# A fused windowed-attention, Fourier-mix and MLP kernel: 1/std moved behind the MLP, the first v loaded in 512-byte runs, the x bounce on ScalarE's DMA queue, w2 loaded at another point

## The chip, the cores and the metric

The kernel runs on one core of one Trainium2 chip. A time is the device time of one execution in microseconds (us); the median of several executions is compared. The engines of the core work beside each other, each through its own instructions in a fixed order, and wait for one another by semaphores: TensorE (PE; its weight loads are listed as PEld), VectorE (DVE), ScalarE (ACT), GpSimd (POOL) and SyncE (SP). A DMA is issued by one of SP, ACT or POOL as an instruction in that engine's order.

## The reference, cut to what matters

```python
# attention: q, k, v of (4 batches, 8 heads, 768 positions, 64)
scores = q @ k.T / 8 + bias                  # bias: minus slope of the head x distance
keep = is_global | is_local                  # the first 8 positions, and the last 96 up to here
a = exp(scores - max) over keep;  a = a / (sum(a) + 1e-9)
x = a @ v                                    # heads side by side: (4, 768, 512)
# mix and MLP
u = x + real(fft(fft(x, axis=1), axis=2))
mu, var = mean(u, -1), mean((u - mu)**2, -1)
un = (u - mu) / sqrt(var + 1e-6)
out = u + maximum(un @ w1, 0) @ w2           # w1 (512, 2048), w2 (2048, 512)
```

All inputs and the output are float32. A positive factor of a row passes through the maximum: maximum(s * un @ w1, 0) @ w2 is s times the value without s.

## The kernel before, in words

**Stages of a batch.** The four batches run one after the other, overlapped. For a batch, the heads are taken in four pairs (hp 0 to 3). q and k of a pair are loaded in float32 (`load`, `qk_dma`, L342), cast to float16 (`cast_qk`, L353 on ACT, L355 on DVE, L357 on POOL), transposed on TensorE (`trans`, L397) and copied out of PSUM (`qkT`, L403). `score` makes the scores of two blocks of 128 keys at a time (L437) and ACT takes the exponential. In batch 0 the distance bias is added in PSUM by a matmul with `sid` (the identity times -8 slope, made on POOL, L964), and the exponential is final (`ex`, L463). From batch 1 on the exponential (`er`, L460) is multiplied by a mask `mk` on DVE (L475); `mk` is made once, by 8 ACT steps (L957). v is loaded in float32 (L317) and cast into `v16` by POOL (`cast_v`, L368). `v_global` and `glob` (L486, L511) serve the 8 global keys. `av` multiplies with v (L547, L560), and DVE divides by the sum (L579, L580), which gives x.

**How v lies.** `v16` has partition p of a block hold the position 2m + t, where p = 64 t + m: the even positions in the lower half and the odd ones in the upper. v is therefore loaded by two DMAs, one for each t, in runs of one position: 64 floats, 256 bytes. q and k are loaded in runs of two positions, 512 bytes, by one DMA over all 128 partitions.

**The bounce.** The Fourier part along the positions wants x in two layouts: the one in which attention leaves it, and one with six adjacent positions in a partition, which is added to the mix to make u. The second comes by way of DRAM (`bounce`): two halves of x are written to `xd` (L598, two DMAs each) and read back as `xr` (L605, L606). All are issued by SP.

**Mix.** DVE folds x (`fold_s`, `fold_d`, L623 to L692), TensorE makes `py` (L712, L715), ACT or DVE copies it to `zy` (L728, L730), POOL mirrors part of it (L748 to L761), TensorE makes `pu` (L792). A batch has three row pairs of 2 x 128 rows (c = 3 b + 0, 1, 2). For each, DVE adds `pu` and `xr` to u (L809), takes the statistics (L818, L820), POOL makes 1/std and -mean/std (L825 to L828), ACT or DVE makes un (L838, L840), TensorE transposes it (L856) and ACT or DVE copies it to `unT` (L864, L866).

**MLP.** For each c, 8 groups `ph` (8 matmuls each, L884), evacuated with the maximum by ACT or DVE (L890, L891), and two outputs of 4 parts `pg` (L907, 4 matmuls each). DVE adds u (L918), SP stores (L922). PSUM has two buffers for `ph`, two for `pg` and two for everything else (batch 0 has two more, `C` and `D`, before the MLP's exist).

**The order of the work.** The order on each engine is fixed when the kernel is built, by a planner (class `Plan`). Each step is handed to it (`later`) with the engines that may do it and a cost for each, the names of what it needs, a latency, and a rank that decides between steps that could start at the same time. The planner keeps a clock for each engine and one for DMA, and takes what could start first; TensorE's units come from four streams (mix, attention, ph, pg), with ten units looked ahead in the first two. On the chip only true data dependencies are waited for: a need that is no data dependency (such as the `gate` in `load`, which holds the loads of batch 1 until `xr` of batch 0) shapes the order, and nothing else.

**Weights.** w1 and w2 are loaded as float16 by four POOL DMAs each (`wload`, L989, L992), w1 after the third v cast, w2 after the first 1/std in the planner's order.

Of the kernel before, what the change touches and what calls it, by code (L numbers as in the profile page):

```python
# [14 lines left out]
P = 128  # L15


class Plan:
# [9 lines left out]
    def __init__(self):  # L28
        self.t = {"PE": 0.0, "ACT": 0.0, "DVE": 0.0, "POOL": 0.0, "SP": 0.0, "DMA": 6.0}
        self.tok = {}  # L30
        self.ready = []
        self.pending = []
        self.rings = {}
        self.left = {}
        self.n = 0
# [49 lines left out]
    def emit(self, place):  # L85
# [6 lines left out]
        if dma:  # L92
            end = self.t["DMA"] = max(self.t["DMA"], end) + dma
# [78 lines left out]
def kernel(  # L172
# [132 lines left out]
    def load(b, hp, which):  # L305
# [4 lines left out]
        gate = [("xr", 0)] if HP <= n < HP + 4 else []  # L310
        if which == "v":
# [32 lines left out]
    def cast_qk(b, hp, w, src, freed):  # L344
# [14 lines left out]
        if b:  # L359
            ways = [("ACT", act(768), lambda: cast("ACT")), ("POOL", 1.6, lambda: cast("POOL"))]  # L360
        pl.later(ways, [("ld", "qk", n, w)] + free("qk", n), 0.0, [("qk", n, w)], [("free",) + freed],
                 rank=1 if b else 0)

# [12 lines left out]
    pl.users(("CD",), 3 * HP + 4 + 3 * NP + len(YG) + NP)  # L376
# [11 lines left out]
    def trans(b, hp):  # L388
        n = HP * b + hp

        def run(start, ring):
# [12 lines left out]
            pl.later([("DVE", dve2(2 * S), evac)], free("qkT", n), e, [("qkT", n)], ring=ring, rank=RA(b))  # L404
# [10 lines left out]
    def score(b, hp, g):  # L415
        n = HP * b + hp
        idx = 3 * (n - HP) + g
# [63 lines left out]
    def v_global(b, halves):  # L481
# [15 lines left out]
        ATT.append(([("v", b, 2 * half + i) for half in halves for i in range(2)] + [("one", 0)], BANKS(b), run))  # L497
# [34 lines left out]
    def av(b, part, jp):  # L532
# [4 lines left out]
        needs += [("v", b, hp) for hp in part]  # L537
# [51 lines left out]
    def bounce(b):  # L589

        for half in range(2):
            def wr(half=half):
# [4 lines left out]
                for t in range(2):  # L597
                    nc.sync.dma_start(rows[t], X[b][64 * t:64 * t + 64, :, c])  # L598
            pl.later([("SP", 0.9, wr)], [("x", b, hp, jp) for hp in (2 * half, 2 * half + 1) for jp in range(NP)] + [("xw", b, 0)][:half], 0.0,
                     [("xw", b, half)], [("free", "x", b)], lat=1.6, dma=2.0)  # L600

        def rd():
            XR[b] = buf("xr", b, [P, NS, Dm], FP16, 3)
            rows = XD[b].rearrange("(m r) d -> m r d", r=6)
            nc.sync.dma_start(XR[b][:, 0:3], rows[:, 0:3])  # L605
            nc.sync.dma_start(XR[b][:, 3:6], rows[:, 3:6])  # L606
        pl.later([("SP", 0.9, rd)], [("xw", b, 0), ("xw", b, 1)] + free("xr", b), 0.0, [("xr", b)], lat=1.6, dma=3.0)
# [170 lines left out]
    MV = {}  # L778
    UNT = {}

    def u_unit(b, pr):
# [4 lines left out]
        def run(start, ring):  # L786
# [20 lines left out]
            def add():  # L807
                u = UT[c] = buf("u", HP + c, [P, 2, Dm], FP32, 2)
                VT(u.rearrange("p a (n r) -> p a n r", r=4), pu.rearrange("p a (r n) -> p a n r", r=4),  # L809
                   XR[b][:, r0:r1 + 1:r1 - r0, :].rearrange("p a (n r) -> p a n r", r=4), op=ALU.add)  # L810
# [280 lines left out]
```

## Time and profile before

| | |
|---|---|
| median of three runs | 302.56 us (302.5 to 303.51) |
| profiled execution | 302.04 us, span 299.9 us |
| busy in the span: PE, DVE, ACT, POOL | 268.0, 183.3, 137.3, 65.8 us |
| mean granted clock of TensorE | 0.952 |
| DMA moved | 37.03 MB, of 66089 packets 26640 under 512 B |
| bounce writes, issue to landing | 2.9 to 10.1 us, median 3.8 |
| first v, issue to landing | 4.9 to 7.7 us, median 6.5 |

A line of the trace names the line of the kernel, the engine, the operation and the tiles that it writes and reads. "Idle before" is time in which that engine did nothing ahead of the instruction, and the releaser is what ended it. A stretch is read together with its clock: matmuls at a granted clock of 0.6 take longer, and the busy time of TensorE then holds less work. SPq and POOLq are the issue of DMAs by these engines.

### The profile page before, as it was taken

The page shows a single profiled execution, that of the slowest core. Times are in us where ns is not written, and L with a number is a line of the kernel's source. Part 1 is how long each engine was busy: PE and PEld are TensorE (multiplying, and loading weights), DVE is VectorE, ACT ScalarE, POOL GpSimd, SP SyncE. Part 2 cuts the span into 40 slices and gives each one's busy share as a digit, 9 for nine tenths or more (in the row PEclk, how much of TensorE's full clock was granted, in tenths as well). Part 3 has the DMA queues.
Part 4 walks back from the last instruction along what each step waited for, and adds up shares of the span by engine and source line. Part 5 has one row for each costly group of instructions (what it writes and reads, how often), then busy time and mean ns, then how long its engine had stood idle before and what let it go on. Part 6 is the DMA issues. An engine that isn't in the chain of part 4 may idle for free.

```text
span 299.9 us, 5827 instructions
## 1 busy us (share of the span) xinstructions
PE 268.0 (89%) x2388; PEld 174.3 (58%) x2388; DVE 183.3 (61%) x350; ACT 137.3 (46%) x189; POOL 65.8 (22%) x151
## 2 busy tenths in 40 slices
PE   2996474899999999559999999999999999999994
PEld 2353353586765546348678565686567758767541
DVE  1476879757556895874667958865688675100111
ACT  2388333675882233176745434658234135434100
POOL 3643015901212137151001125300000431000000
PEclk9999669599999999759999999999999999999998
DMA  8999969999799999330304511100053110100111
GB/s 191 236 229 205 267 201 206 218 217 221 142 214 221 196 264 240 134 107 8 99 0 106 188 42 37 71 2 0 3 142 124 48 39 35 37 1 36 70 70 70
DMA packets 66089, 37.03 MB, mean 123 GB/s; under 512 B 26640, under 2 KB 61712, under 8 KB 66064
## 3 DMA queue, kind: packets, MB, share of 16 engines
q1 hardware_dynamic: 61840, 32.48, 46.1%
q0 software_dynamic: 4224, 4.19, 8.5%
q8 instruction: 18, 0.29, 0.5%
q14 instruction: 7, 0.06, 0.1%
HBM read 31.42 MB, written 9.44 MB: 136 GB/s over the span
## 4 chain that ended last, share of the span: by engine, by line
PE 66%; DVE 12%; DMA 10%; SPq 6%; ACT 2%; POOL 1%; issue 1%; POOLq 0%; DVEq 0%
PE ph L884 26%; PE pg L907 23%; DMA qs<-in_k_dram 5%; PE pav L560 4%; PE sc L437 3%; SPq L317 3%; DMA u<-in_v_dram 2%; DMA xr<-xd 2%; PE pu L792 2%; PE pav L547 2%; SPq L342 2%; PE py L712 2%; DVE st L818 2%; PE ptu L856 2%; DVE u L809 2%; PE pt L397 1%
## 5 line engine op out<-in xcount | busy, mean ns | idle before, releaser
L884 PE MATMUL ph<-unT,w 128*128 128x256 f16 x768 | 97.6, 278 | 1.1 <-ACT unT L864 1.1
L907 PE MATMUL pg<-w,hT 128*128 128x512 f16 x384 | 90.8, 380 | 0.0
L884 PEld LDWEIGHTS <-w 128*128 128x128 f16 x768 | 72.8, 99 | 18.6 <-issue 6.5
L890 ACT ACTIVATE hT<-ph 128x512 f16<-128x512 f32 x69 | 41.2, 597 | 54.5 <-PE ph L884 54.4
L907 PEld LDWEIGHTS <-hT 128*128 128x128 f16 x384 | 36.2, 98 | 35.8 <-issue 1.1
L460 ACT ACTIVATE er<-sc 128x992 f16<-128x992 f32 (+2 forms) x36 | 33.0, 921 | 18.1 <-PE sc L437 11.6
L918 DVE TENSOR_TENSOR ob<-pg,u 128x512 f32<-128x512 f32 x24 | 16.5, 689 | 39.5 <-PE pg L907 37.8
L891 DVE TENSOR_SCALAR hT<-ph 128x512 f16<-128x512 f32 x27 | 18.7, 691 | 22.7 <-PE ph L884 22.5
L353 ACT ACTIVATE qk<-qs 128x768 f16<-128x768 f32 x23 | 18.8, 839 | 19.7 <-PE pt L397 7.9
L475 DVE TENSOR_TENSOR ex<-er,mk 128x992 f16<-128x992 f16 (+2 forms) x36 | 22.4, 635 | 4.1 <-ACT er L460 4.1
L761 POOL COPY ww<-zy 128x512 f16<-128x512 f16 x16 | 9.3, 612 | 54.6 <-PE py L712 37.5
L437 PE MATMUL sc<-qkT 64*128 64x256 f16 (+1 forms) x192 | 19.0, 282 | 0.6 <-DVE qkT L403 0.5
L728 ACT ACTIVATE zy<-py 128x512 f16<-128x512 f32 (+1 forms) x12 | 9.6, 810 | 20.3 <-PE py L715 17.5
L403 DVE COPY qkT<-pt 128x1536 f16<-128x1536 f16 x16 | 15.2, 950 | 5.7 <-PE pt L397 5.7
L838 ACT ACTIVATE un<-u,rstd 128x512 f16<-128x512 f32 x15 | 11.7, 809 | 15.1 <-POOL rstd L828 15.1
L560 PE MATMUL pav<-v,ex 128*128 128x65 f16 x352 | 18.3, 196 | 0.2 <-ACT er L460 0.2
L408 POOL COPY kG<-qkT 64x8 f16<-64x8 f16 x32 | 8.8, 276 | 41.0 <-DVE qkT L403 40.0
L397 PE MATMUL pt<-ident,qk 128*128 128x128 f16 x192 | 15.6, 236 | 2.4 <-ACT qk L353 1.4
L580 DVE TENSOR_TENSOR x<-pav,rc 128x512 f16<-128x512 f32 (+1 forms) x27 | 17.1, 632 | 0.9
L712 PE MATMUL py<-t,ww 128*128 128x256 f16 x48 | 11.7, 298 | 6.1 <-DVE ww L677 5.7
L809 DVE TENSOR_TENSOR u<-pu,xr 128x1024 f32<-128x1024 f32 x12 | 14.5, 1216 | 3.8 <-PE pu L792 3.7
L560 PEld LDWEIGHTS <-ex 128*128 128x128 f16 x352 | 13.3, 98 | 5.3 <-issue 0.6
(87 smaller groups left out, 283.9 us busy)
## 6 DMA issues: line engine op xcount, KB each, us to landing
out_dram<-ob SPq DMA_DIRECT2D x24, 256.0 KB, 2.0
qs<-in_q_dram SPq DMA_DIRECT2D x13, 384.0 KB, 6.6
qs<-in_k_dram SPq DMA_DIRECT2D x13, 384.0 KB, 6.5
vs<-in_v_dram SPq DMA_DIRECT2D x24, 192.0 KB, 7.1
w<-in_moe_w_ch_dram POOLq DMA_DIRECT2D x8, 512.0 KB, 10.3
xd<-x SPq DMA_DIRECT2D x16, 192.0 KB, 3.9
xr<-xd SPq DMA_DIRECT2D x8, 384.0 KB, 3.8
u<-in_v_dram SPq DMA_DIRECT2D x8, 192.0 KB, 6.5
```

The source lines that it names most:

```text
L353: A(d, s, AF.Copy)
L397: nc.tensor.transpose(o[:, j % 2], src[:, w, j].rearrange("p h d -> p (h d)"), idn)
L437: nc.tensor.matmul(pa[:, s, c0:c0 + cw], TT[n][lo:lo + 64, 1, i * P:(i + 1) * P], TT[n][lo:lo + 64, 0, i * P:i * P + cw], start=(b > 0), s ...
L460: A(mine(), cut(pa), AF.Exp, 0.0, 0.125)
L475: VT(o, mine(), m, op=ALU.mult)
L560: nc.tensor.matmul(po[:, jj, hh * 65:(hh + 1) * 65], lhsT, v16[b % 2][:, i, h, 0:65], start=(jp == 0 and a == 0), stop=(a == len(ops) - 1) ...
L712: nc.tensor.matmul(o, wr, t1_sb[:, rs, 128:384], start=True, stop=(wi is None))
L809: VT(u.rearrange("p a (n r) -> p a n r", r=4), pu.rearrange("p a (r n) -> p a n r", r=4), XR[b][:, r0:r1 + 1:r1 - r0, :].rearrange("p a (n ...
L884: nc.tensor.matmul(ph[:, a * CH:(a + 1) * CH], w1[:, d, jb * P:(jb + 1) * P], UNT[c][:, d, :], start=(d == 0), stop=(d == ND - 1))
L890: pl.later([("ACT", act(512), lambda: A(dst, ph, AF.Relu)), ("DVE", dve(512), lambda: V.tensor_scalar_max(dst, ph, 0.0))], [], e, [("h", c ...
L891: ("DVE", dve(512), lambda: V.tensor_scalar_max(dst, ph, 0.0))],
L907: nc.tensor.matmul(pg, HT[c][:, jb, t * P:(t + 1) * P], w2[:, jb, :], start=(jb == 0), stop=(jb == NJ - 1))
```

## The change: what it does, and the diff

Five things are changed together.

- **Normalisation.** u is made by two scalar_tensor_tensor steps of 512 columns, each of which also gives the sum of its row; a small DVE step makes -mean/16 of it. un becomes (u - mean)/16, without 1/std. ACT squares un and sums the squares; POOL makes 1/std (with the factor 16) from that in two steps. The last sum becomes `pg` x (16/std) + u. bn_stats, bn_aggr and two of POOL's four steps go.
- **First v.** The v of batch 0 is loaded like q and k, one DMA in runs of 512 bytes. It is cast to float16 (POOL, DVE or ACT) into a buffer of the `er` tag, and 12 matmuls of 64 x 64 blocks of the identity (`v_place`) put even and odd positions where `v16` wants them; two copies for each head pair (ACT or DVE) bring it there.
- **Bounce.** All writes and reads of the bounce are issued by ACT; the read is one DMA instead of two. The loads of batch 1 get the first write of batch 0's second half as their gate instead of `xr`.
- **Order.** The planner's clocks start otherwise and have a second DMA clock for ACT; `mk` is made after the last x of batch 0; `sid` is made by DVE; casts of batch 0 may go to POOL and `qkT` copies of batch 0 to ACT.
- **Weights.** w1 follows the last k of batch 0, w2 the second v of batch 1, in the planner's order.

```diff
-        self.t = {"PE": 0.0, "ACT": 0.0, "DVE": 0.0, "POOL": 0.0, "SP": 0.0, "DMA": 6.0}
+        self.t = {"PE": 0.0, "ACT": 0.0, "DVE": 0.0, "POOL": 0.0, "SP": 0.7, "DMA": 1.5, "DMA2": 0.0}
...
-            end = self.t["DMA"] = max(self.t["DMA"], end) + dma
+            q = "DMA2" if eng == "ACT" else "DMA"
+            end = self.t[q] = max(self.t[q], end) + dma
...
-        gate = [("xr", 0)] if HP <= n < HP + 4 else []
-        if which == "v":
+        gate = [("xw", 0, 1)] if HP <= n < HP + 4 else []
+        if which == "v" and b == 0:
+            def run():
+                t = buf(vtag, vi, [P, 2 * NS, Dh], FP32, 1)
+                stage[("v", n)] = t
+                qk_dma(t.rearrange("p (j t) d -> p j (t d)", t=2), v, b, h0)
+            pl.later([("SP", 0.45, run)], free(vtag, vi), 0.0, [("ld", "v", n)], lat=1.6, dma=1.2)
+        elif which == "v":
...
+        else:
+            ways += [("POOL", 1.02, lambda: cast("POOL"))]
...
+    def cast_v0(hp):
+        def cast(on):
+            V0[hp] = buf("er", hp, [P, 2, 3, 2, Dh], FP16, 1)
+            d, s = V0[hp].rearrange("p h n t d -> p (h n t) d"), stage[("v", hp)]
...
+        pl.later([("POOL", 0.9, lambda: cast("POOL")), ("DVE", dve2(768), lambda: cast("DVE")),
+                  ("ACT", act(768), lambda: cast("ACT"))],
+                 [("ld", "v", hp)] + free("er", hp), 0.0, [("vc", hp)], [("free",) + stage[("vs", hp)]], rank=0)
+
+    def v_place(hp):
+
+        def run(start, ring):
+            pv = bank(ring, f"pvp_{hp}")
+            for n in range(3):
+                for a in range(2):
+                    for t in range(2):
+                        o = pv[64 * t:64 * t + 64, a, n * P:(n + 1) * P]
+                        nc.tensor.matmul(o.rearrange("p (h d) -> p h d", h=2), idn[64 * a:64 * a + 64, 64 * a:64 * a + 64],
+                                         V0[hp][64 * a:64 * a + 64, :, n, t, :], start=True, stop=True,
+                                         tile_position=(64 * a, 64 * t))
...
+            for a in range(2):
+                dst = v16[0][:, a::2, 2 * hp:2 * hp + 2, 0:Dh]
+                src = pv[:, a, 0:3 * P].rearrange("p (n h d) -> p n h d", h=2, d=Dh)
+                pl.later([("ACT", act(384), lambda dst=dst, src=src: A(dst, src, AF.Copy)),
+                          ("DVE", dve(384), lambda dst=dst, src=src: V.tensor_copy(dst, src))],
+                         [], e, [("v", 0, hp, a)], rank=RA(0), then=freed)
+        ATT.append(([("vc", hp), ("c", "id")], BANKS(0), run))
...
-            pl.later([("DVE", dve2(2 * S), evac)], free("qkT", n), e, [("qkT", n)], ring=ring, rank=RA(b))
+
+            def evac_act():
+                TT[n] = buf("qkT", n, [P, 2, S], FP16, 6)
+                A(TT[n], pt[:, :, 0:S], AF.Copy)
+            pl.later([("DVE", dve2(2 * S), evac)] + [("ACT", act(2 * S), evac_act)] * (b == 0), free("qkT", n), e, [("qkT", n)], ring=ring, rank=RA(b))
...
-                    nc.sync.dma_start(rows[t], X[b][64 * t:64 * t + 64, :, c])
-            pl.later([("SP", 0.9, wr)], [("x", b, hp, jp) for hp in (2 * half, 2 * half + 1) for jp in range(NP)] + [("xw", b, 0)][:half], 0.0,
-                     [("xw", b, half)], [("free", "x", b)], lat=1.6, dma=2.0)
+                    nc.scalar.dma_start(rows[t], X[b][64 * t:64 * t + 64, :, c])
+            pl.later([("ACT", 1.2, wr)], [("x", b, hp, jp) for hp in (2 * half, 2 * half + 1) for jp in range(NP)] + [("xw", b, 0)][:half], 0.0,
+                     [("xw", b, half)], [("free", "x", b)], lat=1.6, dma=2.5)
...
-            nc.sync.dma_start(XR[b][:, 0:3], rows[:, 0:3])
-            nc.sync.dma_start(XR[b][:, 3:6], rows[:, 3:6])
-        pl.later([("SP", 0.9, rd)], [("xw", b, 0), ("xw", b, 1)] + free("xr", b), 0.0, [("xr", b)], lat=1.6, dma=3.0)
+            nc.scalar.dma_start(XR[b], rows)
+        pl.later([("ACT", 0.5, rd)], [("xw", b, 0), ("xw", b, 1)] + free("xr", b), 0.0, [("xr", b)], lat=1.6, dma=4.0)
...
+    SC = 2.0 ** -4
...
-                VT(u.rearrange("p a (n r) -> p a n r", r=4), pu.rearrange("p a (r n) -> p a n r", r=4),
-                   XR[b][:, r0:r1 + 1:r1 - r0, :].rearrange("p a (n r) -> p a n r", r=4), op=ALU.add)
-            pl.later([("DVE", dve(1024), add)], [("xr", b)] + free("u", HP + c), e, [("u", c)],
+                sm = MV[c] = wk.tile([P, 2, 2], FP32, tag="sm", name=f"sm_{c}", bufs=4)
+                for a, rr in enumerate((r0, r1)):
+                    V.scalar_tensor_tensor(u[:, a].rearrange("p (n r) -> p n r", r=4),
+                                           pu[:, a].rearrange("p (r n) -> p n r", r=4), 1.0,
+                                           XR[b][:, rr].rearrange("p (n r) -> p n r", r=4),
+                                           op0=ALU.mult, op1=ALU.add, accum_out=sm[:, a, 0:1])
+                V.tensor_scalar_mul(sm[:, :, 1], sm[:, :, 0], -SC / Dm)
+            pl.later([("DVE", 2 * dve(512) + 0.15, add)], [("xr", b)] + free("u", HP + c), e, [("u", c)],
...
-                    V.bn_stats(st[:, a, :], UT[c][:, a, :])
...
-                nc.gpsimd.tensor_scalar_mul(r[:, :, 1], r[:, :, 1], -1.0)
...
+                m = MV[c][:, a, 1:2]
                 if on == "ACT":
-                    A(cell[0][:, a], UT[c][:, a], AF.Identity, r[:, a, 1:2], r[:, a, 0:1])
+                    A(cell[0][:, a], UT[c][:, a], AF.Identity, m, SC)
...
+            def square(a):
...
+                A(wk.tile([P, Dm], FP16, tag="junk", name=f"j_{c}_{a}", bufs=1), x, AF.Square, accum_out=ss[0][:, a])
+            for a in range(2):
+                pl.later([("ACT", 0.85, lambda a=a: square(a))],
+                         [("un", c, a)], 0.0, [("ss", c, a)], [("free", "un", 1 + c)], rank=2)
+
+            def rstd():
+                r = MV[(c, "r")] = wk.tile([P, 2], FP32, tag="rstd", name=f"rstd_{c}", bufs=4)
+                nc.gpsimd.tensor_scalar(r, ss[0][:, :, 0], 1.0 / Dm, SC * SC * 1e-6, op0=ALU.mult, op1=ALU.add)
+                nc.gpsimd.tensor_tensor(r, r, mhalf, op=ALU.pow)
...
-                VT(cell[0], pg, UT[c][:, t, :], op=ALU.add)
+                V.scalar_tensor_tensor(cell[0], pg, MV[(c, "r")][:, t:t + 1], UT[c][:, t, :],
+                                       op0=ALU.mult, op1=ALU.add)
...
-            pl.later([("ACT", 2 * act(NM), m)], [("c", "dist"), ("x", 0, 1, 0)], 0.0, [("mk", hp)], [("free", "un", 0)], rank=3)
+            pl.later([("ACT", 2 * act(NM), m)], [("c", "dist"), ("x", 0, 3, 2)], 0.0, [("mk", hp)], [("free", "un", 0)], rank=3)
...
-            needs = [("v", 0, 2)] if i == 0 else [("rstd", 0)] if i == 4 else [("wl", i - 1)]
+            needs = [("ld", "qk", 3, 1)] if i == 0 else [("ld", "v", HP + 1)] if i == 4 else [("wl", i - 1)]
```

63 lines of the change are left out of this document (36 added, 27 removed).

## The prediction

> **What bounds the kernel now.** I read the page first, then the busy time by stages, then the instructions in order of time around the two stages that stand out. The stages, cut where the first and the second batch enter the MLP (columns: stretch, its length, busy time of PE, weight loads, DVE, ACT, POOL, granted clock, DMA share, GB/s):
>
> ```profile
> span 299.9 us, 5827 instructions
> 0.00:45.00 45.00, 30.48 (x282) 16.38 (x282) 27.26 (x80) 22.62 (x30) 14.71 (x36) 0.89 1.08 221
> 45.00:54.60 9.60, 3.81 (x53) 3.04 (x52) 8.69 (x16) 4.30 (x6) 6.24 (x14) 0.89 1.27 214
> 54.60:120.00 65.40, 64.46 (x581) 41.35 (x581) 44.12 (x72) 34.49 (x46) 19.97 (x39) 0.96 1.07 214
> 120.00:132.60 12.60, 5.76 (x60) 4.58 (x58) 11.04 (x21) 5.93 (x8) 5.21 (x15) 0.66 0.43 142
> 132.60:296.00 163.40, 163.40 (x1422) 108.94 (x1419) 91.48 (x161) 70.00 (x101) 19.64 (x51) 0.99 0.18 55
> ```
>
> From 132.6 to 296 TensorE is never idle, at a clock of 0.99: what is saved there on another engine is worth nothing. Time can be won in two places only: the 54.6 us before the first MLP matmul, and the hole at 120 to 132.6 where TensorE is busy 5.76 of 12.6 us at a clock of 0.66. The first hole is latency and loads; DMA is at a share above 1 throughout.
>
> The first batch, in order of time (start, length, what; in brackets the idle time before and its releaser):
>
> ```profile
> 21.95 0.56 DVE L355 CAST qk<-qs 128x768 f16<-128x768 f32 x1 [0.43 <-DMA qs<-in_k_dram]
> 26.07 0.22 PE L486 MATMUL pvg<-v,ident 128*32 128x64 f16 x2 [1.84 <-POOL v L368]
> 26.73 1.36 ACT L957 ACTIVATE mk<-un 128x640 f16<-128x640 f16 x2
> 26.75 0.39 PE L437 MATMUL sc<-qkT 64*128 64x256 f16 x4
> 28.12 1.00 ACT L463 ACTIVATE ex<-sc 128x992 f16<-128x992 f32 x1
> 33.72 0.42 DVE L580 TENSOR_TENSOR x<-pav,rc 128x256 f16<-128x256 f32 x1
> 34.17 1.27 SPq L598 DMA_DIRECT2D xd<-x  x2
> 39.83 0.33 SPq L605 DMA_DIRECT2D xr<-xd  x1
> 40.68 0.43 SPq L342 DMA_DIRECT2D qs<-in_q_dram  x1
> 44.98 1.23 DVE L809 TENSOR_TENSOR u<-pu,xr 128x1024 f32<-128x1024 f32 x1 [0.86 <-PE pu L792]
> 48.03 1.28 DVE L818 BATCH_NORM_STATS2 st<-u 128x6 f32<-128x512 f32 x2
> 51.29 1.52 ACT L838 ACTIVATE un<-u,rstd 128x512 f16<-128x512 f32 x2 [2.27 <-POOL rstd L828]
> 54.58 1.86 PE L884 MATMUL ph<-unT,w 128*128 128x256 f16 x8 [1.11 <-ACT unT L864]
> ```
>
> The last k lands at 21.95, TensorE then stands 1.84 us for the cast of the last v, x is complete at 34.14, and 6.3 us pass between the first u (44.98) and its un (51.29). The second batch:
>
> ```profile
> 98.85 0.69 DVE L580 TENSOR_TENSOR x<-pav,rc 128x512 f16<-128x512 f32 x1
> 107.24 2.29 SPq L598 DMA_DIRECT2D xd<-x  x2
> 114.96 2.82 SPq L605 DMA_DIRECT2D xr<-xd  x1
> 116.29 1.06 PE L792 MATMUL pu<-t,zy 128*128 128x128 f16 x16
> 121.80 2.36 DVE L809 TENSOR_TENSOR u<-pu,xr 128x1024 f32<-128x1024 f32 x2 [0.15 <-DMA xr<-xd]
> 128.00 0.52 DVE L840 TENSOR_SCALAR un<-u,mv,rstd 128x512 f16<-128x512 f32 x1
> 132.55 1.91 PE L884 MATMUL ph<-unT,w 128*128 128x256 f16 x8
> ```
>
> x is complete at 99.54, but SyncE issues its second half only at 107.24, 7.7 us later, behind loads and stores of its in-order queue; pu is there at 117.35 and u waits for xr until 121.80. From u to un pass 6.2 us, and TensorE has run out of MLP work meanwhile.
>
> **The change, part by part.**
>
> *v in longer runs.* DMA rates in 40 equal parts of the first 30 us (0.75 us each), and the groups that price the new work:
>
> ```profile
> GB/s 0 0 61 276 343 317 298 272 152 184 173 275 290 285 237 158 180 180 287 290 283 223 156 192 190 290 289 282 224 163 191 192 200 186 208 213 215 214 215 218
> L397 PE MATMUL pt<-ident,qk 128*128 128x128 f16 x192 | 15.6, 236 | 2.4 <-ACT qk L353 1.4 <-ACT er L460 0.9
> L728 ACT ACTIVATE zy<-py 128x512 f16<-128x512 f32 x6 | 3.5, 596 | 11.0 <-PE py L715 8.2 <-PE py L712 1.4 <-DVE zy L730 1.4
> L820 DVE BATCH_NORM_AGGREGATE mv<-st 128x2 f32<-128x6 f32 x24 | 3.6, 173 | 0.0
> L838 ACT ACTIVATE un<-u,rstd 128x512 f16<-128x512 f32 x15 | 11.7, 809 | 15.1 <-POOL rstd L828 15.1
> L918 DVE TENSOR_TENSOR ob<-pg,u 128x512 f32<-128x512 f32 x24 | 16.5, 689 | 39.5 <-PE pg L907 37.8 <-DMA out_dram<-ob 1.6
> 30.00:40.00 10.00, 4.33 (x45) 2.88 (x45) 8.81 (x33) 2.88 (x4) 0.00 (x0) 0.60 0.95 221
> ```
>
> The plateaus near 285 GB/s are q and k, the dips near 170 are v. A v of 393 KB takes 2.3 us at 170 and 1.4 us at 285; it now has the layout of q and k, so I take their rate: about 1.0 us less for each, 3.0 before the last k and 4.0 before the last v (bounds: 0 if the dips had another cause; 1.3 each, up to the 343 of the best part). The four v need one issue on SyncE instead of two each.
>
> The 1.84 us that TensorE stood for the last v go, as v lands earlier and in step with k. In its place come a cast, 12 small matmuls and two evacuations for each head pair. Twelve matmuls of the row L397 at its mean 0.24 us would be 2.8 us laid end to end, but they overlap; I take 1 us per pair. An evacuation of 384 columns lies below the 0.60 us of the 512-column row. That is 4 us on TensorE and 4.8 us shared by ACT and DVE, in 45 us with 14.5 us free on TensorE and 22 on ACT, so most is hidden; without that cover it would be some 9 us. I charge 1.5 us (0 to 5). The mask exponentials (L957) are put off until x is complete: one of them held ACT from 26.73 while the score for the next exponential was there at 27.14, so 1.0 us goes; they fall into the stretch that is now 30 to 40 us, where ACT has work for 2.88 us (last row). The sid products move from POOL to DVE, 8 operations, in the same cover. Sum up to x: -3.0 - 1.84 - 1.0 + 1.5 = **-4.3 us**, x near 29.8.
>
> *The statistics.* Out go 24 statistics, 24 aggregates, and four POOL steps in a chain between u and un. In come, per pair of rows, two adds of 512 instead of one of 1024 (0.69 each by the row L918, some overlap: 1.3), two accumulator reads and one product. The trace has no accumulator read: between 0 and the smallest DVE step above, 0.17; I take 0.17, so 0.5 us for the three. u to un becomes 1.3 + 0.5 + 0.2 of hand-overs = 2.0 us instead of 6.3 and 6.2: **-4.3** in batch 0, **-4.2** in batch 1 (-2.3 if the planner puts the next pair's add between, -4.8 if the reads are free). The squares are 24 new ACT steps of 0.81 us, 19.4 us; nothing waits for them but 1/std, and that only the last sum, a whole MLP of its rows later. The last sum stays one DVE step of 0.69.
>
> *The bounce on ScalarE.* Batch 1: write issued at 99.6 + 2.3, landed 5.4 later (109.53 to 114.96), read landed 6.84 later (114.96 to 121.80): 114.1, before pu at 117.35. The whole wait of **-4.4** goes (0 to -4.4). In batch 0 the same two legs took 34.17 to at most 44.98, 10.8 us: x at 29.8 gives xr at 40.6 where u is due at 40.7. That is no slack, and the loads of batch 1 now stand behind nothing on SyncE and run beside it: +0.5 (0 to 3). Each bounce also costs ACT its issues; they, and ACT's wait for the landing, are what is queued ahead of its evacuations:
>
> ```profile
> SPq L605 <- DMA xd<-x: 9.7, 4, 3.7
> L598 SPq DMA_DIRECT2D xd<-x x16: 580/618/1608, 21.6 to 221.7; - x16
> L890 ACT ACTIVATE hT<-ph 128x512 f16<-128x512 f32 x69 | 41.2, 597 | 54.5 <-PE ph L884 54.4
> ```
>
> 16 x 0.62 = 9.9 us of issue, and 9.7 us in which SyncE stood for the write to land. In the last stage ACT has 70.0 + 15 (squares) + 10 of 163.4; I charge 1.0 us in all for TensorE stops (0 to 6).
>
> Against this edit speaks the Trainium skill, "DMA: Bandwidth & Descriptors", section "Issuing engines are not separate DMA queues": transfers from any issuing engine interleave on the same 16 DMA engines, and another issuer saves only sequencer time. By it the landing times stay, and they stay in my sum as well; but the 7.7 us of waiting in SyncE's order is neither of the two, and this trace shows it.
>
> *Loads of batch 1 and w2.* The first of them went out at 40.68, behind the read of xr. Now nothing on SyncE holds them but free buffers. As DMA is saturated, an earlier issue helps only by the transfer time set free: 4 us of v, and w2 taken out of the way of the later loads. Its price shows in the chain of waits:
>
> ```profile
> 55.29 16.48 DMA qs<-in_k_dram
> ...
> qs<-in_k_dram SPq DMA_DIRECT2D x13, 384.0 KB, 6.5
> ```
>
> Against the median of 6.5 us for such a load (the page's last part), 10 us were lost to w2 and its neighbours. I take 7 us for the whole attention of batch 1 (4 from v alone, 11 with most of w2's 10).
>
> **Sum.** First MLP matmul: 54.58 - 4.3 - 4.3 + 0.5 = 46.5. From there TensorE needs 77.97 us to batch 1's MLP today, of which 7.8 idle (0.94 + 6.84) and 2.0 lost to the clock (0.34 x 5.76): 68.2 at best, so 114.7. The chain of batch 1 gives 132.55 - 7 - 4.4 - 4.2 = 117.0. The later one counts: **-15.6**. After that the same 163.4 us and tail, +1.0. The profiled execution took 302.04 (span 299.9 and 2.1 around it): 302.04 - 14.6 = 287.4, and as the median of the runs stands 0.5 higher, **288**.
>
> **Rivals.**
>
> 1. *The loads of batch 1 don't come earlier* (DMA was the bound and stays it; w1 now shares with them). Batch 1's MLP starts at 132.55 - 8.6 = 124.0; time 302.56 - 7.6 = 295. For it: share above 1 until 75 us. Against: v and w2 give bandwidth back. 0.20.
> 2. *The read of xr stays late*, since the two legs land as slowly beside the loads that now run ahead: -15.6 + 4.4 + 1.0, 292.4. For it: the 6.84 us that the read took. Against: 3.2 us of slack. 0.10.
> 3. *ScalarE's queue is blocked: slower.* ACT's order is fixed beforehand; it stands at the write until x is there and at the read until the write has landed, and PSUM evacuations stand behind it, so TensorE stops. All of 9.7 us of waits, 9.9 of issue and 1.3 for four reads of 0.33 would be 21 us: 302.56 - 15.6 + 21 = 308. It decides against the change once some 15 of the 21 reach TensorE. For it: 69 of the 96 MLP evacuations are on ACT (row L890). Against: ACT has room for more than half the last stage, and the planner lets an evacuation go to DVE. 0.13.
> 4. *The squares switch ACT's tables.*
>
> ```profile
> L353 ACT ACT_TABLE_LOAD x1 | 1.3, 1283 | 0.7 <-PEq L1072 0.7
> ```
>
> One load serves four functions now, the exponential among them. If a square needed another table, 24 squares between exponentials bring up to 48 loads, 62 us on ACT, many in front of evacuations: over 310. Against: three of the functions sharing the one load are as simple as a square. 0.02. The Trainium skill, "ScalarE: Activation LUTs", section "Table sets: the hidden batching unit", has cheap functions in every set, but does not name the square there; no run here shows it yet.
>
> **How the numbers follow.** My forecast, both holes closing, has 0.55, with its own range of 281 to 291: the low end is the TensorE bound with 2.3 us more and the start at its better bounds; the high end has 4 us of loads and 1 us more of stops. Rivals 1 and 2 are faster too: 0.85 in all. Within 0.5% (301.0 to 304.1, about what a measurement can tell from no change) is the lighter part of rival 3, 0.04; slower is its rest and rival 4, 0.11. The range 280 to 300 leaves out slightly over 0.15.
>
> **What would show it.** First MLP matmul near 46.5; DMA dips of the first 20 us gone; the wait of u for xr in batch 1 gone, and un 2 us after u; TensorE idle between the batches below 3 us; ACT with one table load. Wrong would be: ACT idle time put down to the landing of xd with evacuations late behind it, a new hole of TensorE in the long last stage, or the loads of batch 1 ending as late as now.

## The result, and the profile after

The changed kernel takes 294.1 us (median of 4 runs, 293.86 to 295.24) against 302.53 for the kernel before in the same comparison: a ratio of 0.9732, 95% interval 0.9686 to 0.9777. The forecast was 288 with a range of 280 to 300. Its profiled execution took 294.05 us, with a span of 292.1 and a granted clock of 0.965; the one before 302.04, 299.9 and 0.952. Ratios, here and below, leave out executions that were more than 1.5% slower than the fastest of the same kernel, among them two of the four of norm_alone and one of the four each of undo_v and b0sp_w2spread.

Busy time by stages of the kernel after, cut where its first two batches enter the MLP and 12.6 us before the second does (columns as in the prediction):

```profile
0.00:56.70 56.70, 36.41 (x396) 22.18 (x397) 36.26 (x108) 32.43 (x47) 16.51 (x40) 0.85 1.03 236
56.70:112.50 55.80, 52.84 (x489) 33.98 (x488) 41.94 (x69) 28.03 (x42) 16.97 (x26) 0.97 1.06 211
112.50:125.07 12.57, 12.57 (x124) 8.75 (x122) 10.75 (x23) 7.46 (x13) 5.57 (x12) 1.00 0.42 125
125.07:288.00 162.93, 162.93 (x1435) 109.87 (x1432) 93.29 (x179) 74.82 (x122) 19.48 (x45) 1.00 0.19 62
```

The second hole is gone: in the 12.57 us before batch 1's MLP TensorE is busy throughout and at full clock, and in the long last stage it still never stops. The first hole is still there, and no shorter. The first batch in order of time:

```profile
18.88 0.56 DVE L362 CAST qk<-qs 128x768 f16<-128x768 f32 x1 [0.69 <-DMA qs<-in_k_dram]
...
24.24 0.84 PE L453 MATMUL pt<-ident,qk 128*128 128x128 f16 x12
...
33.04 0.42 DVE L640 TENSOR_TENSOR x<-pav,rc 128x256 f16<-128x256 f32 x1
34.99 4.36 ACTq L658 DMA_DIRECT2D xd<-x  x2
39.40 3.87 ACT L1021 ACTIVATE mk<-un 128x640 f16<-128x640 f16 x6 [8.87 <-DMA xd<-x]
43.08 0.35 ACTq L665 DMA_DIRECT2D xr<-xd  x1
46.22 1.06 ACT L787 ACTIVATE zy<-py 128x512 f16<-128x512 f32 x2
50.08 0.69 DVE L871 SCALAR_TENSOR_TENSOR u<-pu,xr 128x512 f32<-128x512 f32 x1 [1.37 <-PE pu L852]
51.70 0.72 ACT L886 ACTIVATE un<-u,sm 128x512 f16<-128x512 f32 x1 [1.63 <-DVE sm L875]
54.55 1.02 ACT L927 ACTIVATE unT<-ptu 128x1024 f16<-128x1024 f16 x1
56.70 1.92 PE L947 MATMUL ph<-unT,w 128*128 128x256 f16 x16
```

The last k is cast 3.1 us earlier than before, x is complete at 33.46 (before 34.14), u begins at 50.08 (before 44.98), un follows it by 1.6 us (before 6.3), and the first MLP matmul comes at 56.70: 2.1 us later than before, not 8 earlier. One sign that the prediction named for being wrong is there: ACT stood idle for 8.87 us, the end of it put down to a DMA of xd, and its copy of py came late behind that. The second batch:

```profile
98.41 0.69 DVE L640 TENSOR_TENSOR x<-pav,rc 128x512 f16<-128x512 f32 x1
99.13 1.26 ACTq L658 DMA_DIRECT2D xd<-x  x2
105.37 0.34 ACTq L665 DMA_DIRECT2D xr<-xd  x1
118.54 0.69 DVE L871 SCALAR_TENSOR_TENSOR u<-pu,xr 128x512 f32<-128x512 f32 x1
120.22 0.49 DVE L888 TENSOR_SCALAR un<-u,sm 128x512 f16<-128x512 f32 x1
125.07 1.91 PE L947 MATMUL ph<-unT,w 128*128 128x256 f16 x16
```

x is complete at 99.10 (before 99.54). The read of xr is issued 9.6 us earlier than before and u waits for it no more: u is 3.3 us earlier, un 7.8 and the MLP 7.5. These 7.5 us are the gain; behind the MLP's start 167.0 us are left, and before there were 167.35.

### The profile page after: what moved, and what is told of

Its sections match the earlier page's. It is cut to its first block, busy times and chain, and to the rows that moved or that the text cites. A ratio compares the mean times of both kernels' runs of the same rounds, so it can differ in the third digit from the quotient of the medians.

```text
span 292.1 us, 5960 instructions
## 1 busy us (share of the span) xinstructions
PE 264.9 (91%) x2436; PEld 174.8 (60%) x2436; DVE 183.0 (63%) x376; ACT 142.7 (49%) x224; POOL 58.5 (20%) x122
## 4 chain that ended last, share of the span: by engine, by line
PE 74%; DMA 16%; SPq 3%; ACT 3%; DVE 1%; issue 1%; ACTq 0%; DVEq 0%
PE pg L970 28%; PE ph L947 27%; DMA qs<-in_q_dram 8%; DMA vs<-in_v_dram 7%; PE pav L620 4%; PE pu L852 3%; PE sc L497 3%; SPq L349 3%; PE pt L453 2%; PE pav L607 2%; PE py L771 2%; PE ptu L919 1%; ACT mk L1021 1%; PE py L774 1%; ACT qk L360 1%; SPq L992 1%
## 5 line engine op out<-in xcount | busy, mean ns | idle before, releaser
L947 PE MATMUL ph<-unT,w 128*128 128x256 f16 x768 | 96.0, 276 | 2.7 <-ACT hT L953 2.7
L953 ACT ACTIVATE hT<-ph 128x512 f16<-128x512 f32 x59 | 35.2, 597 | 47.1 <-PE ph L947 47.1
L981 DVE SCALAR_TENSOR_TENSOR ob<-pg,rstd,u 128x512 f32<-128x512 f32 x24 | 17.9, 748 | 35.8 <-PE pg L970 34.1
L954 DVE TENSOR_SCALAR hT<-ph 128x512 f16<-128x512 f32 x37 | 25.4, 690 | 22.3 <-PE ph L947 22.3
L535 DVE TENSOR_TENSOR ex<-er,mk 128x992 f16<-128x992 f16 (+2 forms) x36 | 23.4, 660 | 2.7 <-ACT er L520 2.6
L360 ACT ACTIVATE qk<-qs 128x768 f16<-128x768 f32 x17 | 14.0, 837 | 18.1 <-PE pt L453 7.1
L871 DVE SCALAR_TENSOR_TENSOR u<-pu,xr 128x512 f32<-128x512 f32 x24 | 15.6, 688 | 5.2 <-PE pu L852 4.9
L468 POOL COPY kG<-qkT 64x8 f16<-64x8 f16 x32 | 7.6, 236 | 53.7 <-DVE qkT L459 45.8
L497 PEld LDWEIGHTS <-qkT 64*128 64x128 f16 x192 | 5.7, 95 | 16.5 <-issue 10.5
L453 PE MATMUL pt<-ident,qk 128*128 128x128 f16 x192 | 14.5, 231 | 1.1 <-ACT unT L927 1.1
```

The lines of the kernel that those rows point to most:

```text
L453: nc.tensor.transpose(o[:, j % 2], src[:, w, j].rearrange("p h d -> p (h d)"), idn)
L497: nc.tensor.matmul(pa[:, s, c0:c0 + cw], TT[n][lo:lo + 64, 1, i * P:(i + 1) * P], TT[n][lo:lo + 64, 0, i * P:i * P + cw], start=(b > 0), s ...
L535: VT(o, mine(), m, op=ALU.mult)
L947: nc.tensor.matmul(ph[:, a * CH:(a + 1) * CH], w1[:, d, jb * P:(jb + 1) * P], UNT[c][:, d, :], start=(d == 0), stop=(d == ND - 1))
L953: pl.later([("ACT", act(512), lambda: A(dst, ph, AF.Relu)), ("DVE", dve(512), lambda: V.tensor_scalar_max(dst, ph, 0.0))], [], e, [("h", c ...
L954: ("DVE", dve(512), lambda: V.tensor_scalar_max(dst, ph, 0.0))],
```

## The experiments

All kernels compute the whole reference. In the table, "start 0" is the first MLP matmul of batch 0 and "start 1" that of batch 1, both in the profiled execution. Ratios are to the kernel before on the same chip, with 95% intervals. The executions of one kernel scatter, in some cases by more than 3 us, and the profiled one is one of them: those of norm_alone, undo_v and b0sp_w2spread were 2.8, 2.6 and 3.8 us below the median of their kernel. So the ratio is the measure, and the times only say where it comes from.

| kernel | ratio | span | start 0 | start 1 | span less start 1 |
|---|---|---|---|---|---|
| before | 1 | 299.9 | 54.58 | 132.55 | 167.4 |
| after | 0.9732 [0.9686, 0.9777] | 292.1 | 56.70 | 125.07 | 167.0 |
| after, again | 0.9773 [0.9720, 0.9827] | 292.9 | 57.18 | 125.87 | 167.0 |
| norm_alone | 0.9856 [0.9792, 0.9919] | 295.0 | 52.64 | 125.33 | 169.7 |
| v_alone | 0.9922 [0.9884, 0.9960] | 296.3 | 53.85 | 128.96 | 167.3 |
| bounce_alone | 1.0041 [1.0016, 1.0065] | 300.7 | 60.16 | 132.30 | 168.4 |
| undo_norm | 1.0411 [1.0324, 1.0499] | 311.9 | 62.67 | 145.98 | 165.9 |
| undo_bounce | 0.9792 [0.9727, 0.9857] | 293.4 | 52.93 | 124.20 | 169.2 |
| undo_v | 0.9706 [0.9638, 0.9774] | 289.9 | 58.08 | 122.61 | 167.3 |
| bounce0_sp | 0.9847 [0.9786, 0.9909] | 293.3 | 52.68 | 125.41 | 167.9 |
| mk_late | 0.9917 [0.9887, 0.9947] | 298.1 | 55.79 | 130.18 | 167.9 |
| w2_late | 0.9926 [0.9891, 0.9961] | 296.8 | 57.16 | 129.25 | 167.5 |
| b0sp_w2late | 0.9670 [0.9619, 0.9720] | 288.9 | 51.25 | 120.20 | 168.7 |
| b0sp_w2spread | 0.9676 [0.9590, 0.9761] | 287.8 | 51.03 | 116.32 | 171.5 |

The last column is nearly a constant, 165.9 to 169.7 with one exception (171.5). Most of what a kernel takes is settled at start 1. And start 0 does not settle start 1: bounce0_sp enters the MLP 4.0 us earlier than the kernel after and reaches start 1 no earlier.

**One part alone.** Each is the kernel before with one part of the change.

norm_alone: the sum from the accumulator, the squares on ScalarE, 1/std at the last sum.

```
-                VT(u.rearrange(...), pu.rearrange(...), XR[b][...], op=ALU.add)
+                    V.scalar_tensor_tensor(u[:, a]..., pu[:, a]..., 1.0, XR[b][:, rr]..., ..., accum_out=sm[:, a, 0:1])
...
-                         [("rstd", c)] + free("un", 1 + c), 0.0, [("un", c, a)])
+                         [("u", c)] + free("un", 1 + c), 0.0, [("un", c, a)])
```

> Only the normalisation is changed. Theory (the gain of the whole change is the shorter way from u to the MLP and the lost wait for xr, both in the second hole): u to un 1.7 us instead of 6.3, first MLP matmul near 50 (54.6 before), and the second batch's MLP about 4 us earlier, as u there still waits for xr until about 122; time 298, between 296 and 300. Rival (the way from u to un is hidden, and the loads decide): first MLP matmul earlier, second batch's unchanged, time 302.

Measured 0.9856. Batch 0 and batch 1 of norm_alone, in order of time:

```profile
45.51 0.69 DVE L812 SCALAR_TENSOR_TENSOR u<-pu,xr 128x512 f32<-128x512 f32 x1 [0.43 <-PE pu L793]
47.15 1.33 ACT L827 ACTIVATE un<-u,sm 128x512 f16<-128x512 f32 x2 [1.44 <-DVE sm L816]
...
111.67 1.49 SPq L605 DMA_DIRECT2D xr<-xd  x1
118.01 0.69 DVE L812 SCALAR_TENSOR_TENSOR u<-pu,xr 128x512 f32<-128x512 f32 x1 [0.38 <-issue]
```

u to un is 1.6 us. The bounce is still on SyncE here, and yet u of batch 1 hardly waits for xr: the read went out 3.3 us earlier than in the kernel before. So the wait that I had given to the bounce goes with the other part too. Start 1 is 7.2 us earlier, where the theory had 4.

v_alone: v of batch 0 in the layout of q and k, placed by TensorE (cast_v0, v_place).

```
-            cast_v(0, hp)
+            cast_v0(hp)
...
+                    v_place(hp)
```

> Only the first v is changed (512-byte runs, cast and placement by TensorE). Theory (the loads get shorter, but the placement takes it back in TensorE's and DVE's order): last k about 3 us earlier, x of batch 0 complete at 33 to 34 as before, time 302 within 1 us. Rival (the earlier v carries through, and in the whole change something else spoilt it): x near 30, first MLP matmul near 50.5, time 302 or, if the loads of batch 1 follow, 298.

Measured 0.9922. x of batch 0 is complete at 34.00, 0.1 us earlier than before, though the last k lands 2.7 us earlier (19.23): the shorter loads bring x nothing, as the theory said. The time is not the theory's: x of batch 1 (complete at 95.91) and start 1 are both 3.6 us earlier. How the change of batch 0's v reaches batch 1 is not shown.

bounce_alone: both halves of the bounce from ScalarE's queue, and batch 1's loads let go when the write has been issued.

```
-                    nc.sync.dma_start(rows[t], X[b][64 * t:64 * t + 64, :, c])
+                    nc.scalar.dma_start(rows[t], X[b][64 * t:64 * t + 64, :, c])
...
-        gate = [("xr", 0)] if HP <= n < HP + 4 else []
+        gate = [("xw", 0, 1)] if HP <= n < HP + 4 else []
```

> Only the bounce goes to ScalarE's queue, with the new gate. Theory (it helps batch 1 and hurts batch 0): the wait of u for xr in batch 1 is gone, 4 us, but the loads of batch 1 now run ahead of batch 0's bounce, and ACT stands at it: first MLP matmul 1 to 4 us later than 54.6; time 298 to 301. Rival (ACT isn't hurt): first MLP matmul at 54.6 or earlier, time 298.

Measured 1.0041, slower by 0.4%, and start 0 is later than theory or rival had it. Batch 0 of bounce_alone:

```profile
34.99 2.08 ACTq L599 DMA_DIRECT2D xd<-x  x2
43.26 0.35 ACTq L606 DMA_DIRECT2D xr<-xd  x1
43.71 0.60 ACT L728 ACTIVATE zy<-py 128x512 f16<-128x512 f32 x1 [9.50 <-PE py L715]
...
51.39 1.22 DVE L809 TENSOR_TENSOR u<-pu,xr 128x1024 f32<-128x1024 f32 x1 [3.97 <-DMA xr<-xd]
```

ACT stands in front of the read until 43.26 and evacuates py only then (before at 41.05); xr lands later still, and start 0 moves by +5.6 us. Batch 1 makes it good: start 1 is at 132.30.

**One part undone.** Each is the kernel after without one part.

undo_norm, the first diff the other way round:

> The changed kernel with the old normalisation (statistics, 1/std ahead of un). Theory (the shorter way from u to un carries the end through batch 1's chain): u to un in batch 1 back at 5 to 6 us, a hole of TensorE of 3 to 5 us near 120, time 297 to 299. Rival (it is hidden, as TensorE had MLP work until 125 in the changed kernel): 294 to 295.

Measured 1.0411: 12 us slower than before, and no theory had that. In order of time, undo_norm:

```profile
55.39 1.52 ACT L897 ACTIVATE un<-u,rstd 128x512 f16<-128x512 f32 x2 [2.35 <-POOL rstd L887]
...
121.72 0.69 DVE L977 TENSOR_TENSOR ob<-pg,u 128x512 f32<-128x512 f32 x1 [3.81 <-DMA out_dram<-ob]
122.47 1.87 PE L966 MATMUL pg<-w,hT 128*128 128x512 f16 x4 [3.38 <-DVE ob L977]
142.28 1.80 PE L915 MATMUL ptu<-ident,un 128*128 128x128 f16 x16 [2.89 <-ACT er L520]
```

Against the kernel after, start 0 is 6.0 us later (2.9 of them between u and un, which waits for POOL's rstd, and 2.3 from un to the matmul). On top of that x of batch 1 loses another 0.7 us (complete at 105.76), u another 5.8 (131.02; a last sum stands for the store that frees its buffer, and TensorE behind it), and start 1 another 8.4 (u to un again; TensorE stands for an exponential that is queued on ACT behind two normalisations and a cast). Together 20.9 us, of which 19.8 are left at the end of the span. So the parts don't add up: alone they are worth -1.4, -0.8 and +0.4%, but without the normalisation the rest of the change makes a kernel 4.1% slower than the one before. Where the 20.9 us lie is shown; why the fixed order loses so much more here than in bounce_alone is not.

undo_bounce, the third diff the other way round:

> The changed kernel with all of the bounce on SyncE and the old gate. Theory (ScalarE's queue helps batch 1 and hurts batch 0, and only batch 1 counts for the end): first MLP matmul near 52, u of batch 1 waits for xr again, time 296 to 298. Rival (the move is a loss on the whole): 292 to 293.

Measured 0.9792; its interval overlaps both of those of the kernel after. Batch 1 of undo_bounce:

```profile
114.02 0.42 SPq L665 DMA_DIRECT2D xr<-xd  x1
117.72 0.69 DVE L872 SCALAR_TENSOR_TENSOR u<-pu,xr 128x512 f32<-128x512 f32 x1
```

The read goes out as late as 114.02, and yet DVE has no idle time in front of u at 117.72. It is a near thing: the first half of xr landed at 117.70. Start 0 is 3.8 us earlier than in the kernel after and start 1 0.9 us earlier. No gain from moving the bounce can be shown.

undo_v, the second diff the other way round:

> The changed kernel with the old first v (256-byte runs, no placement). Theory (the placement takes back what the transfer gains, as x of batch 0 came 0.7 us earlier only): 293.5 to 295.5. Rival (v is worth what it was worth alone, 2.4 us): 296 to 297.

Measured 0.9706, again not to be told from the kernel after. x of batch 0 is complete only at 37.58, 4.1 us later than after, and yet start 0 is only 1.4 us later and start 1 no later. The read of xr goes out 7.3 us behind x here and 9.6 us behind it in the kernel after; why is said under bounce0_sp and mk_late. Beside the other parts, no gain from the longer runs of v can be shown. Of the three parts only the normalisation carries a gain in the whole. The new order, and the new places of w1 and w2, were not undone by themselves.

**The first hole.** bounce0_sp: batch 0's bounce back on SyncE, with batch 1's loads behind it.

```
-        gate = [("xw", 0, 1)] if HP <= n < HP + 4 else []
+        gate = [("xr", 0)] if HP <= n < HP + 4 else []
...
+                    (nc.scalar if b else nc.sync).dma_start(rows[t], X[b][64 * t:64 * t + 64, :, c])
+            pl.later([("ACT", 1.2, wr) if b else ("SP", 0.9, wr)], ...
```

> The changed kernel, but batch 0's bounce is issued by SyncE again, ahead of the loads of batch 1; batches 1 to 3 stay on ScalarE. Theory (ACT's 4.4 us at the write and the wait for its landing delayed batch 0): the copy of py on ACT starts near 42 instead of 46.2, first MLP matmul near 52 instead of 56.7, and as TensorE has no hole of note later, time about 290. Rival (the start is held by the added TensorE and DVE work, not by the bounce): first MLP matmul at 56 to 57, time 294.

Measured 0.9847. Batch 0 first, then what stood at 59 to 120 us (a piece of the chain of waits, and two groups in order of time):

```profile
37.47 0.34 SPq L665 DMA_DIRECT2D xr<-xd  x1
41.27 1.08 ACT L787 ACTIVATE zy<-py 128x512 f16<-128x512 f32 x2 [5.12 <-PE py L774]
```

```profile
58.98 13.47 DMA qs<-in_q_dram
```

```profile
112.28 0.84 ACT L360 ACTIVATE qk<-qs 128x768 f16<-128x768 f32 x1 [3.54 <-DMA qs<-in_k_dram]
114.32 0.75 DVE L981 SCALAR_TENSOR_TENSOR ob<-pg,rstd,u 128x512 f32<-128x512 f32 x1 [3.95 <-DMA out_dram<-ob]
```

The read goes out 5.6 us earlier than in the kernel after, the copy of py is 5.0 earlier and start 0 4.0 earlier: so the bounce, and not the added work, was what held batch 0. The edit also puts batch 1's loads back behind the bounce. But the time is not better, and the hole at the end of batch 1's attention is open again (TensorE busy 8.03 of 10 us from 110 to 120 and 8.05 from 120 to 130), where ACT and DVE stand for a load and a store.

mk_late: the mask exponentials put off until the first u, as they stand ahead of the copy of py in ACT's order.

```
-            pl.later([("ACT", 2 * act(NM), m)], [("c", "dist"), ("x", 0, 3, 2)], ...
+            pl.later([("ACT", 2 * act(NM), m)], [("c", "dist"), ("u", 0)], ...
```

> The changed kernel, but the mask exponentials are put behind the first u instead of behind the last x of batch 0. Theory (ACT is held by the bounce's write and its landing, and then by 5.2 us of masks, before it copies py): without the masks ahead the copy of py starts near 43.4 instead of 46.2, first MLP matmul near 54 instead of 56.7; the end moves little, as the chain of batch 1 sets it: 293 to 294. Rival (the start alone sets the end): 291.

Measured 0.9917: a miss. ACT of mk_late:

```profile
43.36 0.34 ACTq L665 DMA_DIRECT2D xr<-xd  x1
43.83 1.57 ACT L360 ACTIVATE qk<-qs 128x768 f16<-128x768 f32 x2 [13.00 <-DMA xd<-x]
45.31 1.06 ACT L787 ACTIVATE zy<-py 128x512 f16<-128x512 f32 x2
```

The masks had lain in time in which ACT stood for the write's landing anyway: without them the read goes out at 43.36, no earlier, and py is copied only 0.9 us earlier. What holds batch 0 is the write, and what holds the write are loads of batch 1. In the kernel after, with each issue of the write shown by itself (start, length), the time from issue to landing of the second, and two pieces of the chain of waits:

```profile
34.99 0.58 ACTq L658 DMA_DIRECT2D xd<-x  x1
38.77 0.58 ACTq L658 DMA_DIRECT2D xd<-x  x1
```

```profile
xd<-x ACTq DMA_DIRECT2D x1, 192.0 KB, 4.2
```

```profile
18.65 20.10 DMA vs<-in_v_dram
...
38.77 1.99 DMA xd<-x
```

The 4.36 us are no issue time. The two writes take 0.58 us each and start 3.78 us apart, since each waits for a load. In this trace the DMAs of SyncE and ScalarE tell of their landing by eight semaphores that they share and that are used again and again, and these writes wait until the DMA that had their semaphore before has landed. The second write has that of a v load of batch 1, issued at 18.65 and landed at 18.65 + 20.10 = 38.75; it starts 0.02 us later. The first has that of a k load of batch 1 that landed at 34.92, and starts at 34.99, 1.5 us after x was complete. mk_late and undo_norm show the same pair of waits; in undo_v the semaphores were free by then, and the writes start right behind x (37.61, x at 37.58). The second write lands at 38.77 + 4.2 = 43.0, and the read goes out at 43.08. In bounce0_sp, where the loads of batch 1 stand behind the bounce, the two writes start 0.62 us apart and land in 3.0 us. Of the some 5.6 us between the two reads 4.4 are thus the later start of the second write, and 1.3 its slower landing. In bounce_alone the two writes have no such wait (34.99 and 35.61), but beside the loads they take some 7.4 us to land. So it is the loads of batch 1 ahead of the bounce that hold it, by their semaphores or by the transfer. The gate does not hold them on the chip once the write is issued by another engine than they are: the first went out at 16.95.

TensorE is busy only 13.5 of the 20 us from 60 to 80 in mk_late (17.3 in the kernel after). Its longest stop there, 3.45 us, stands for ACT, and ACT for a q load (4.91 us); that the masks, now between the exponentials of batch 1, are the cause is not shown.

**w2.** w2_late: w2 only after the last k of batch 1.

```
-            needs = [("ld", "qk", 3, 1)] if i == 0 else [("ld", "v", HP + 1)] if i == 4 else [("wl", i - 1)]
+            needs = [("ld", "qk", 3, 1)] if i == 0 else [("ld", "qk", 2 * HP - 1, 1)] if i == 4 else [("wl", i - 1)]
```

> The changed kernel, but the four loads of w2 follow the last k of batch 1 in the planner's order instead of its second v. Theory (w2 holds up batch 1's loads: 16.9 us for one q): no q or k load of batch 1 takes over 10 us, TensorE's 2.7 us of idle time near 71 gone, x of batch 1 complete 3 to 6 us before 99; time 290 to 291. Rival (DMA carries the same bytes in another order, and the parts of the MLP with w2 now wait): a hole of TensorE near 65 to 75 and 294 to 296.

Measured 0.9926: a miss too. The chain of waits of the kernel after has a load that runs beside w2 in one piece:

```profile
54.55 16.89 DMA qs<-in_q_dram
```

and behind it TensorE has its only longer stop between start 0 and start 1:

```profile
72.84 2.81 PE L947 MATMUL ph<-unT,w 128*128 128x256 f16 x16 [2.71 <-ACT hT L953]
```

In w2_late, in order of time:

```profile
81.31 0.84 ACT L360 ACTIVATE qk<-qs 128x768 f16<-128x768 f32 x1 [7.34 <-DMA qs<-in_k_dram]
83.09 0.50 PE L497 MATMUL sc<-qkT 64*128 64x256 f16 x4 [6.60 <-ACT er L520]
```

The load that suffers is another one, a k that takes 16.63 us from 64.66 on, and it costs more: ACT stands 7.34 us at its cast, and TensorE 6.60 us behind ACT, where the hole of the kernel after was 2.71. x of batch 1 is complete at 102.30, 3.2 us later than in the kernel after.

b0sp_w2late is both, bounce0_sp and w2_late; after_again, beside it on the same chip, is the kernel after unchanged.

> Both edits: batch 0's bounce on SyncE, w2 behind the last k of batch 1. Theory (two limits stood one behind the other: ACT at batch 0's bounce, then batch 1's loads): first MLP matmul near 52, batch 1's first near 120, time 287 to 290. Rival (batch 1's chain is held by something else, such as ACT's and DVE's order between 100 and 120): first MLP matmul near 52 but batch 1's still at 124 or later, time 292 to 294.

> The changed kernel once more, on the chip of the next three runs, as their measure: 294, ratio 0.973.

Measured 0.9670 [0.9619, 0.9720] and 0.9773 [0.9720, 0.9827]: some 1% faster than the kernel after (0.9670 / 0.9773 = 0.989), with intervals that just touch. Start 0 is at 51.25 and start 1 at 120.20, as the theory had it, though one load still takes 15.71 us in its chain of waits and TensorE is still idle for 6.2 us between the two starts. Of its two halves, one alone brought nothing (0.9847) and the other was slower than the kernel after (0.9926). Why they pay together, when each by itself does not, is not shown.

b0sp_w2spread: the same bounce, and each part of w2 behind a load of its own instead of in one bunch.

```
+            needs = ... else [("ld", "qk", HP + i - 3, 1)] + [("wl", i - 1)] * (i > 4) if i >= 4 else ...
```

> Batch 0's bounce on SyncE, and the four loads of w2 spread: one behind each of the last k of the second, third and fourth head pair of batch 1 and the first of batch 2. Theory (four w2 loads in a row hold one q or k load for 13 to 17 us, and ACT stands at its cast): no q or k load of batch 1 over 11 us, TensorE idle between 60 and 95 below 2 us, time 286 to 289. Rival (DMA is full all the same, only another load is late): 291 to 293.

Measured 0.9676 [0.9590, 0.9761], the same as b0sp_w2late within its interval. No q or k load behind start 0 is in its chain of waits any more; the longest of batch 1 takes 11.5 us. Start 1 comes at 116.32, but 171.5 us are left behind it: work of TensorE that was done ahead of start 1 now lies behind it.

## Why the prediction was right and where it was wrong

The time lies in the range, but not by the sum. The first hole was to give 8.1 us and cost 2.1; from start 0 to start 1 the forecast gave 7.5 us (70.5 instead of 77.97) and 9.6 were won (68.37). That the total still falls in is owed to the width of the range, and to rival 1, which it takes in.

*v in longer runs: the cause was right, the term was not on the path.* DMA rates of the kernel after in the same 0.75 us parts:

```profile
GB/s 0 0 102 279 346 316 260 241 331 314 290 290 290 289 282 284 292 289 292 289 291 289 292 290 298 351 373 356 242 222 218 212 215 218 218 212 215 218 236 221
```

The dips near 170 are gone and the last k is cast 3.1 us earlier, as said (-3.0). But "x near 29.8" failed: x came at 33.46, -0.7 instead of -4.3. The step that failed is the -3.0 itself. The k was cast by 19.44 and its transposition ran at 24.24 with no idle time in front of it: TensorE had other work in its order until then. The kernel before had shown it already; the cast of the last k ended there at 22.51, and its transposition had no idle time in front of it either:

```profile
23.24 0.83 PE L397 MATMUL pt<-ident,qk 128*128 128x128 f16 x12
```

I had taken the last arrival for what x waited for, and the row that I showed was of a DVE that waited 0.43 us, not of TensorE. The transposition even came 1.0 us later; from it to x it is 9.2 us instead of 10.9, and the wait for the last v is gone, as forecast. With 0 in place of the -3.0 the sum would have been -1.3.

*The bounce in batch 0: mis-sized, and the error with the largest price.* I charged +0.5 (0 to 3). From x to u it took 16.6 us instead of 10.8: +5.8. I had let rival 3, ScalarE blocked, act in the long last stage, where it cost nothing (TensorE 162.93 of 162.93). It acted in batch 0: ACT stood for two loads of batch 1 before its two writes, then for the landing, and the copy of py was queued behind both. bounce0_sp and bounce_alone show it from both sides. The two turn the queue and the order of the loads together, so no run separates them; the trace puts the delay of the write on the loads that ran ahead (18.65 to 38.75), and ScalarE's part is that the copy of py stood behind it. The Trainium skill ("DMA: Bandwidth & Descriptors", section "Issuing engines are not separate DMA queues") says that transfers of all issuing engines share the same DMA engines, so that another issuer wins no transfer time. The trace agrees: beside loads that SyncE had issued, ScalarE's writes landed in 4.2 us (after) and some 7.4 us (bounce_alone), and SyncE's own, ahead of those loads, in 3.0 us (bounce0_sp).

*The statistics: right.* u to un is 1.6 and 1.7 us where I said 2.0: -4.7 and -4.5 for -4.3 and -4.2. From un to the first matmul it is 5.0 us instead of 3.3, and that is TensorE's order:

```profile
53.90 0.61 PE L919 MATMUL ptu<-ident,un 128*128 128x128 f16 x8
55.62 0.83 PE L453 MATMUL pt<-ident,qk 128*128 128x128 f16 x12 [1.11 <-ACT unT L927]
```

un is ready at 52.4, but its transposition stands behind `pu` of the next row pair until 53.90, and behind unT a transposition and a score of batch 1 go ahead of the MLP, until 56.70. Two squares and a cast of ACT lie in between as well, 52.33 to 54.52, but the transposition of un ends only at 54.51, so nothing shows a wait for the squares.

*First MLP matmul 46.5: measured 56.70.* The 10.2 us are 3.6 (x), 5.3 (the bounce), 1.7 (un to the matmul), less 0.4 (statistics).

*TensorE's bound, 68.2 at best: that it was 68.37 is luck.* TensorE was still idle for 2.96 us of them (forecast: below 3), so its work was 65.4 us; and undo_v (64.53) and b0sp_w2spread (65.29) stay below 68.2. My sum had left out that the clock was 0.96 in the first 65.4 us, and that the order decides how much of the work lies ahead of start 1. The second hole is closed, as forecast. Whether the early error went through to the end is open: bounce0_sp takes 4.0 us of it back at start 0 and is no earlier at start 1, while b0sp_w2late is earlier at both.

*The loads of batch 1, -7: measured -0.4* (x at 99.10). Rival 1 said this, and its 295 is what came. With w2 in a bunch, some load of q or k took 13 to 17 us wherever the bunch was put (the kernel after, bounce0_sp, w2_late, b0sp_w2late), and in the kernel after and w2_late ACT stood for it; spread out (b0sp_w2spread), the longest took 11.5 us. But b0sp_w2late, with such a load, is as fast as b0sp_w2spread, so what the bunch costs the whole is not shown.

*The xr wait, -4.4: gone, but it gave 2.9, and not by the bounce alone.* u came 3.3 us earlier, of which x gave 0.4. The wait is as good as gone in norm_alone, v_alone and undo_bounce too, where SyncE issues the read. And 114.96, which I read as the landing of the write before, was SyncE's order again: the write had landed by 112.6.

*Stops in the long stage, +1.0: none (the stage behind start 1 is 0.3 us shorter). One table load: right.* Groups of the kernel after:

```profile
L360 ACT ACT_TABLE_LOAD x1 | 1.3, 1283 | 0.7 <-PEq L1139 0.7
L898 ACT ACTIVATE j<-un 128x512 f16<-128x512 f16 x24 | 14.9, 623 | 0.6 <-POOL rstd L905 0.3
L898 ACT ACTIVATION_READ_ACCUMULATOR j<-un 128x1 f32 x24 | 4.5, 188 | 0.0
L871 DVE DVE_READ_ACCUMULATOR u<-pu,xr 128x1 f32 x24 | 2.0, 83 | 0.0
```

The 24 squares took 19.4 us with their reads, the predicted sum, and rival 4 is refuted: the square is served by the table that is there.

## What to carry to other kernels

An arrival is a bound only if the engine of the critical work stood idle in front of its consumer; look for that idle time before pricing the arrival. Where two limits lie in series, here batch 0's latency and the loads of batch 1, mending one may show nothing (bounce0_sp) or do harm (w2_late), and both together pay. A DMA issued from a compute engine costs that engine its issue, its waits, and everything queued behind these; here it waited for earlier loads that had used the same semaphores. Price it in the stage where DMA is saturated, not where it is free, and ask which loads run ahead of it once they are issued by another engine.

## What the runs showed of the hardware that was not expected

A DMA waited for another with which it shares no data: ScalarE's two writes in batch 0 stood 1.5 and 3.2 us for two loads of SyncE that had used their semaphores before, and each started less than 0.1 us after the load had landed. Their own issue took 0.58 us each, and 0.58 and 0.64 us at 99.13. On SyncE the listed length of an issue did vary, 0.37 to 9.35 us for a q or k load, and a v load of batch 1 that had no semaphore to wait for took 2.32 us at 22.88; the long ones lay where DMA was saturated (share 1.03 and 1.06 up to 112.50). Reading an accumulator cost DVE 83 ns, half of what I took, and ACT 188 ns.
